# Attention: a batch is ranked two steps earlier in an even unit, and its fourth map scatter goes to an odd unit's fifth step

## The chip, the cores and the metric

The kernel runs on one core of a Trainium2 chip. The core has a tensor engine (PE; its weight loads are shown apart, as PEld), a vector engine (DVE), a scalar engine (ACT), a general engine (POOL) and a queue engine that issues transfers (SP). Each works through its own instructions in order, and they wait for one another by semaphores. The metric is the device time of one execution in microseconds.

## The reference, cut to what matters

```python
scores = cap * np.tanh(q @ k.T / sqrt(64) / cap)       # 8 batches, 12 heads, 448 x 448
attn   = exp(scores - max); attn /= attn.sum(-1)
x      = (attn @ v), heads side by side                # 3584 tokens x 768
logits = x @ w_gate + modality_bias[modality_id]       # 8 experts
e_idx  = argmax(logits); gate_w = softmax(logits)[e_idx]
out[t] = gate_w[t] * (relu(x[t] @ w1[e]) @ w2[e])      # e = e_idx[t]
```

Every token goes to one expert, so the tokens have to be sorted by expert between the two halves.

## The kernel before, in words

The attention is cut into 24 units `d`, each of four heads of one batch (three units make a batch). A unit has seven steps `s` of 64 keys, and the loop in `attention` goes through all 168 steps `n`. Each step puts these on the engines: four score products on PE (`scores`, line 542, `sc`), a tanh and, for two steps together, two exponentials on ACT (lines 547 and 549, `pt`), an add of the weights for the softmax's sums on DVE (`add`, line 562, `tot`), four steps behind, and the weighing of the values on PE (`weigh`, line 574, `xT`), four to six steps behind by a table. The last weighing of a unit falls into the fourth step of the next one, and a copy of `xT` on DVE follows it (`keep`, line 581).

For each pair of units, PE makes the logits in an even unit's sixth step (`sums2`, lines 613 and 615, `glog`) and transposes them in the next odd unit's fifth step (`turn2`, line 604, `lt`); DVE takes the reciprocals and scales the logits (lines 632 and 655). When a batch's three units are through, `route` ranks its 448 tokens: it is a Python generator cut by `yield`, which `start_route` starts in an odd unit's sixth step and `go_on` takes one piece further. Its pieces are:

- the sum of the logits (line 286), then the maximum and the one-hot choice `oh` (lines 294 to 313), in an odd unit's sixth and seventh step
- the running counts: three adds into `before` and one into `acc` (lines 319 and 320), and the gate (lines 300 to 302)
- the rank: two small products on PE, of `oh` (line 326) and of `before` (line 328), then five small DVE instructions to each token's row in a map (`rows`, `posf`, `pos`, lines 332 to 340), and scatters of the map's entries by POOL (line 346, `mapd`). For batches 0 to 4 only three of the four scatters are issued there; the fourth, with a cast of its own (line 360), is put into `self.rest` and issued later.

Instructions marked with `pin` keep the order in which the program writes them; the others of `route` are put in by a scheduler. The order that results is shown in the section on the change. After the attention, from about 300 us on, the experts' layers run, and PE works there without a break.

The calls that the change touches are these, in the loop of the steps:

```python
if s == 1 and d % 2 == 0 and self.rest:            # line 745: the fourth scatter
    self.rest.pop()()
if s in ((1,), (1, 6))[d % 2] and d != SOON + 2:   # line 747: a piece of route
    go_on()
...
for m in due[n]:                                   # line 764: the weighing of this step
    weigh(m)
...
if s == 3 and d % 2 == 0 and d != SOON + 2:        # line 768: a piece of route
    go_on()
```

Of the kernel before, what the change touches and what calls it, by code (L numbers as in the profile page):

```python
# [92 lines left out]
class Program:  # L93
# [414 lines left out]
    def attention(self, firsts, rp, xp):  # L508
        tc, nc = self.tc, self.nc
        pe, pin, V = nc.tensor, self.pin, nc.vector  # L510
        with ExitStack() as st:
# [10 lines left out]
            def fetch(d):  # L522
                if d < ND:
                    for g in (2 * d, 2 * d + 1) if d else ():
                        self.load_kq(ring[g % 4], g)
                    vas[d] = ld.tile([128, VW], F32, name="va")
                    self.load(vas[d], self.v[d // NU, d % NU])
# [6 lines left out]
            def scores(n):  # L534

                d, s = divmod(n, STEPS)
                sc = ps_s.tile([128, 2, 512], F32, name="sc")
                for i in range(2):
                    kq = ring[(2 * d + i) % 4]
                    for j in range(2):  # L540
                        rows = slice(j * D, (j + 1) * D)
                        pin(pe.matmul(  # L542
                            sc[i * KB : (i + 1) * KB, j, :S], kq[rows, S + s * KB : S + (s + 1) * KB], kq[rows, :S],
                            start=True, stop=True,
                        ))
                slow = n // STEPS == SOON + 2 and 2 <= n % STEPS <= 5
                pin(nc.scalar.activation(weights(n), sc[:, :, :S], AF.Tanh, scale=self.isc if slow else self.iscr))  # L547
                for m in (n - 1, n) if n % 2 else ():
                    pin(nc.scalar.activation(weights(m), weights(m), AF.Exp, scale=self.cabsr))  # L549
# [57 lines left out]
            def sums2(a, copy=V.tensor_copy):  # L607

                glog = self.glog = ps_g.tile([128, 512], F32, name="glog", tag="glog")
                group = lambda x: glog[x * GW : (x + 1) * GW, :S]  # L610
                every = [(u, g) for u in range(2) for g in range(2)]
                for u, g in every:
                    pin(pe.matmul(group(2 * u + g), self.pick2, tots[a + u][:, g], start=True, stop=False))
                for u, g in every:
                    pin(pe.matmul(
                        group(2 * u + g), self.wgt[:, (2 * (a + u) + g) % NP], kept[a + u][:, g], start=False, stop=True
                    ))
                gls[a] = xp.tile([128, S], F32, name="gl", bufs=2)
                pin(copy(gls[a], glog[:, :S]))
# [8 lines left out]
            def turn2(a):  # L628

                lt = flip(gls.pop(a))  # L630
                for u in range(2):
                    pin(V.reciprocal(recs(a + u), lt[:, :, 2 * u : 2 * u + 2, GE : GE + 2]))
                    lts[a + u] = lt[:, :, 2 * u : 2 * u + 2]
# [12 lines left out]
            def logits(d):  # L646

                b, r = divmod(d, NU)
                lt = lts.pop(d)
                rec = self.recips(pays[b])  # L650
                if r == 0:
                    lgs[b] = xp.tile([CP, C, H, E], F32, name="lg", bufs=2)
                for i in range(2):
                    h0 = 4 * r + 2 * i
                    pin(V.tensor_tensor(
                        lgs[b][:, :, h0 : h0 + 2], lt[:, :, i, :GE].rearrange("p c (j e) -> p c j e", j=2),
                        rec[:, :, :, 2 * r + i].unsqueeze(3).to_broadcast([CP, C, 2, E]), op=ALU.mult,
                    ))
# [10 lines left out]
            def store(b, queue=nc.sync):  # L669
                xs = xss.pop(b).rearrange("p m k b -> p m (k b)")  # L670
                wide = KC * HB
                for g in range(4):
                    j, h = divmod(g, 2)
                    o = (2 * h + j) * wide
                    put = queue.dma_start(
                        self.xd[b * S : (b + 1) * S, o : o + wide].rearrange("(m a) f -> a m f", a=HB),
                        xs[g * HB : (g + 1) * HB],
                    )
                    if queue is nc.sync:
                        self.last_sp = pin(put).ins  # L680
# [9 lines left out]
            def go_on():  # L690
                for way in routing:
                    next(way, None)
# [12 lines left out]
            SOON = (B - 1) * NU - 1  # L705
            END = STEPS * ND
            due = [[] for _ in range(END + 1)]
            for m in range(END):
                d, s = divmod(m, STEPS)
# [3 lines left out]
            def more(n, count=0):  # L713
                nonlocal added
                while (n not in held or count > 0) and added <= n - BEHIND + (n >= END - STEPS):
                    add(added)
                    added += 1
                    count -= 1
                    if count == 0:
                        break  # L720
# [3 lines left out]
            for n in range(END):  # L724
                d, s = divmod(n, STEPS)
                if s == 0:
                    fetch(d + 1)
                    if 1 < d < SOON and d % NU == 1:
                        store(d // NU - 1)
                    if d == 0:  # L730
                        self.fetch_bias()
                        self.fetch_cap()
                    if d == 1:
                        self.blank(xp.tile([128, FF], F32, name="spare", bufs=2))
                    if 0 <= d - 2 < CLEAR:
                        self.empty_map(d - 2)
                scores(n)
                late = False
                if not late:
                    more(n)  # L740
                if (d, s) == (1, 3):
                    self.gate_bias()
                if (d, s) == (1, 4):
                    self.columns()
                if s == 1 and d % 2 == 0 and self.rest:
                    self.rest.pop()()
                if s in ((1,), (1, 6))[d % 2] and d != SOON + 2:
                    go_on()
                if s == 4 and d % 2 and 3 <= d < PAIRED + 3:
                    turn2(d - 3)  # L750
                    go_on()
                    logits(d - 3)
                    logits(d - 2)
                if s == 5 and d % 2 == 0 and 2 <= d <= PAIRED:
                    sums2(d - 2)
                if (d, s) == (SOON + 1, 5):
                    sums(SOON)
                if s == 5 and d % 2 and 3 <= d < PAIRED + 2:
                    for u in (d - 3, d - 2):
                        if u % NU == NU - 1:  # L760
                            start_route(u // NU)
                if (d, s) == (SOON + 2, 2):
                    more(n, 1)
                for m in due[n]:
                    weigh(m)
                    if m % STEPS == STEPS - 1:
                        keep(m // STEPS)
                if s == 3 and d % 2 == 0 and d != SOON + 2:
                    go_on()
                if s == (2 if d % 2 else 4) and d % NU == 2:  # L770
                    tokens(d - 2)
                if s == (4 if d == SOON + 1 else 6) and 0 < d < ND - 1 and d % NU != 1:
                    tokens(d - 1)
                    if d == SOON + 1:
                        store(d // NU - 1)
                if d == SOON + 2 and s in (3, 4):
                    more(n, {3: 2, 4: 9}[s])
                if (d, s) == (SOON + 1, 6):
                    turn(SOON)
                    logits(SOON)  # L780
                    start_route(SOON // NU, firm=True)
                    go_on()
                    go_on()
                if (d, s) == (SOON + 2, 1):
                    go_on()
                    meta = self.early_slot(self.cpool, self.ps_r)
                    self.first_e = self.expert(meta, 0)
                    load_w1((0, 1), self.first_e)
                if (d, s) == (SOON + 2, 4):
                    maps = self.rows(meta, 0)  # L790
                    got = self.gather(maps, known=NT - S)
                    load_w1((2, 3, 4, 5), self.register(nc.gpsimd, meta[0:1, 0:1], E - 1, got.ins), nc.gpsimd)
                if d == SOON + 3 and s >= STEPS - TW:
                    self.norm(maps, s - (STEPS - TW))
# [818 lines left out]
```

## Time and profile before

| | us |
|---|---|
| median of three runs (lowest, highest) | 786.42 (786.34, 788.58) |
| profiled execution: time, and its span | 786.07, 784.5 |
| PE busy | 772.2 (98%) |
| PE weight loads busy | 580.0 (74%) |
| DVE busy | 524.3 (67%) |
| ACT busy | 500.0 (64%) |
| POOL busy | 238.4 (30%) |

The span goes from the first to the last instruction. A busy share is an average over two halves that differ: by the page's slices ACT is nearly full up to about 290 us and half idle after it, while PE is full in both. The trace splits each of PE's f32 products of 448 columns into two, so the four products of a step are eight there. A row of a timeline gives the start, the duration from the first of the merged instructions to the end of the last, the engine, line, tiles and count, and in brackets the engine's idle time before it and what ended that. Instructions of one engine overlap a little, so a row's end can lie behind the start of the next.

### The profile page before, as it was taken

The numbers are of one execution on the slowest core, as the hardware profiler recorded it, in microseconds if no ns is written. First come the engines' busy times: TensorE is split into PE (matmuls) and PEld (weight loads), VectorE is DVE, ScalarE is ACT, GpSimd is POOL, SyncE is SP. The second block draws the span as 40 slices with busy tenths as digits, with TensorE's granted clock in tenths as the row PEclk, the third lists the DMA queues.
The fourth block names the chain that finished last, engine by engine and source line by source line (L and its number), as shares of the span: only waits on it lengthen the run. The fifth ranks groups of instructions, "written<-read, shape, count | busy, mean of one in ns | idle before, by whom it ended". The sixth has DMA issues, their size and how long they took to land. (4 is left out here: it accounts for less than half of the span.)

```text
span 784.5 us, 15421 instructions
## 1 busy us (share of the span) xinstructions
PE 772.2 (98%) x5811; PEld 580.0 (74%) x5811; DVE 524.3 (67%) x899; ACT 500.0 (64%) x704; POOL 238.4 (30%) x259
## 2 busy tenths in 40 slices
PE   7999999999999999999999999999999999999996
PEld 2343333343333337999999999999999999998985
DVE  4778897888798898965826448265482664727830
ACT  7999999999999895454533445235443354436630
POOL 3000121022122140248560723607427064015202
PEclk9999999999999999999999999999999999999999
DMA  6366545262544664598444563455634655346772
GB/s 201 115 205 204 163 144 182 102 213 94 192 141 146 165 219 154 141 311 277 157 138 176 191 229 131 142 202 185 201 124 157 228 174 183 109 176 207 244 283 98
DMA packets 58951, 139.33 MB, mean 178 GB/s; under 512 B 9025, under 2 KB 25814, under 8 KB 58867
## 3 DMA queue, kind: packets, MB, share of 16 engines
q1 hardware_dynamic: 48512, 113.32, 44.3%
q0 software_dynamic: 10352, 24.94, 9.4%
q8 instruction: 47, 0.77, 0.4%
q14 instruction: 38, 0.30, 0.1%
q10 hardware_dynamic: 2, 0.00, 0.0%
HBM read 114.47 MB, written 24.34 MB: 177 GB/s over the span
## 5 line engine op out<-in xcount | busy, mean ns | idle before, releaser
L549 ACT ACTIVATE pt<-pt 128x896 f32<-128x896 f32 x168 | 152.2, 972 | 0.0
L547 ACT ACTIVATE pt<-sc 128x896 f32<-128x896 f32 x164 | 145.6, 938 | 9.9 <-PE sc L542 9.6
L574 PE MATMUL xT<-pt,va 64*64 64x448 f32 x1344 | 149.8, 537 | 0.1
L1111 PE MATMUL py<-bh,hh 128*128 128x384 f32 (+1 forms) x440 | 147.9, 336 | 0.1
L1111 PE MATMUL py<-bh,hl 128*128 128x384 f32 (+1 forms) x440 | 147.5, 335 | 0.0
L1111 PE MATMUL py<-bl,hh 128*128 128x384 f32 (+1 forms) x440 | 147.5, 335 | 0.0
L1054 PE MATMUL ph<-x,al 128*128 128x384 f32 (+1 forms) x456 | 147.3, 323 | 0.0
L957 POOL DMA_INDIRECT xg<-xd,at x92 | 112.3, 1221 | 112.1 <-DVE look L1275 85.0
L562 DVE TENSOR_TENSOR tot<-tot,pt 128x896 f32<-128x896 f32 x118 | 127.8, 1083 | 9.2 <-ACT pt L549 3.4
L1050 PE MATMUL ph<-x,ah 128*128 128x384 f32 x360 | 120.6, 335 | 0.0
L1051 PE MATMUL ph<-x,ah 128*128 128x384 f32 x360 | 120.3, 334 | 0.0
L346 POOL DMA_INDIRECT mapd<-pay,pos x32 | 39.8, 1245 | 244.7 <-DVE pos L340 128.6
L574 PEld LDWEIGHTS xT<-pt,va 64*64 64x64 f32 x1344 | 51.1, 133 | 75.5 <-issue 70.8
L995 DVE TENSOR_TENSOR bl<-raw,bh 128x768 fp32r<-128x768 f32 x78 | 72.2, 955 | 39.8 <-ACT bh L994 39.5
L1133 ACT ACTIVATE ot<-py,mt 128x384 f32<-128x384 f32 (+1 forms) x55 | 31.9, 581 | 104.7 <-PE py L1111 93.8
L1054 PEld LDWEIGHTS ph<-x,al 128*128 128x128 f32 x456 | 85.7, 188 | 0.0
L1065 ACT ACTIVATE hh<-ph 128x384 fp32r<-128x384 f32 x63 | 30.6, 489 | 84.9 <-PE ph L1054 80.7
L1111 PEld LDWEIGHTS py<-bh,hh 128*128 128x128 f32 x440 | 82.6, 188 | 1.2 <-ACT ot L1133 0.5
L1111 PEld LDWEIGHTS py<-bl,hh 128*128 128x128 f32 x440 | 82.6, 188 | 0.3
L1111 PEld LDWEIGHTS py<-bh,hl 128*128 128x128 f32 x440 | 82.6, 188 | 0.3
L542 PE MATMUL sc<-kq 64*64 64x448 f32 x672 | 78.3, 551 | 4.0 <-ACT pt L547 4.0
L542 PE MATMUL sc<-kx 64*64 64x448 f32 x672 | 78.5, 540 | 0.1
(245 smaller groups left out, 972.9 us busy)
## 6 DMA issues: line engine op xcount, KB each, us to landing
raw<-in_w_dram SPq DMA_DIRECT2D x81, 384.0 KB, 4.7
raw<-in_w_dram SPq DMA_DIRECT2D x48, 512.0 KB, 4.5
va<-in_v_dram SPq DMA_DIRECT2D x24, 448.0 KB, 5.7
kx<-in_kq_dram SPq DMA_DIRECT2D x24, 448.0 KB, 3.8
xd<-xs SPq DMA_DIRECT2D x32, 336.0 KB, 6.8
kq<-in_kq_dram SPq DMA_DIRECT2D x22, 448.0 KB, 4.0
raw<-in_w1q_dram SPq DMA_DIRECT2D x12, 512.0 KB, 7.6
mapd<-spare SPq DMA_DIRECT2D x4, 480.0 KB, 8.1
```

The source lines that it names most:

```text
L346: put = nc.gpsimd.indirect_dma_start(self.mapd, bass.IndirectOffsetOnAxis(ap=pos, axis=0), pay[:, c, :], None, bounds_check=E * RG - 1, oo ...
L542: pin(pe.matmul(sc[i * KB : (i + 1) * KB, j, :S], kq[rows, S + s * KB : S + (s + 1) * KB], kq[rows, :S], start=True, stop=True,))
L547: pin(nc.scalar.activation(weights(n), sc[:, :, :S], AF.Tanh, scale=self.isc if slow else self.iscr))
L549: pin(nc.scalar.activation(weights(m), weights(m), AF.Exp, scale=self.cabsr))
L562: pin(V.tensor_tensor(tots[d], pt_of(n - 1) if s == 1 else tots[d], pt_of(n), op=ALU.add))
L574: pin(pe.matmul(self.xT[j * D : (j + 1) * D, i, :S], vas[d][rows, o : o + D], pt[rows, j], start=s == 0, stop=s == STEPS - 1,))
L957: got = self.nc.gpsimd.indirect_dma_start(self.xg.rearrange("p t f -> p (t f)")[:, g * QW : (g + 1) * QW], None, self.xd.rearrange("n (q c ...
L995: keep((minus or self.nc.vector).tensor_tensor(lo, raw, hi, op=ALU.subtract))
L1050: keep(nc.tensor.matmul(ph[:, :w], hi[:, fs], self.x[:, k, 0, :w], start=first, stop=False))
L1051: keep(nc.tensor.matmul(ph[:, :w], hi[:, fs], self.x[:, k, 1, :w], start=False, stop=False))
L1054: self.done = keep(nc.tensor.matmul(ph[:, :w], lo[:, fs], self.x[:, k, 0, :w], start=False, stop=last)).ins
L1111: got = nc.tensor.matmul(pys[half][:, :wide], self.h[a][:, f, rows], self.w2s[f][c][:, cs], start=f == i == 0, stop=f == FC - 1 and i == 2,)
```

## The change

In an even unit, the piece of `route` that makes the counts is called in the first step in place of the second, and the piece that ranks is called in the second step, ahead of the weighing, in place of the fourth, behind it. The fourth scatter is issued in an odd unit's fifth step, ahead of the transposes' reciprocals, in place of an even unit's second.

```diff
-                if s == 1 and d % 2 == 0 and self.rest:
+                if s == 4 and d % 2 and self.rest:
                     self.rest.pop()()
-                if s in ((1,), (1, 6))[d % 2] and d != SOON + 2:
+                if s in ((0, 1), (1, 6))[d % 2] and d != SOON + 2:
                     go_on()
...
-                if s == 3 and d % 2 == 0 and d != SOON + 2:
-                    go_on()
```

Six batches are ranked there (0 to 5). On PE, batch 0's first four steps of the even unit stand like this before (`sc` are scores, `xT` the weighing; each row of scores or weighing is one step's four products, or two steps'):

```order
L542 MATMUL sc<-kq 64x448 x4
L574 MATMUL xT<-pt,va 64x448 x8
L542 MATMUL sc<-kq 64x448 x4
L574 MATMUL xT<-pt,va 64x448 x4
L542 MATMUL sc<-kq 64x448 x4
L574 MATMUL xT<-pt,va 64x448 x4
L326 LDWEIGHTS tri
L326 MATMUL rank<-oh,tri 112x32
L328 LDWEIGHTS ones
L328 MATMUL rank<-before,ones 112x32
L542 MATMUL sc<-kq 64x448 x8
```

The first row is the second step's scores. With the change, the same place of PE's order:

```order
L542 MATMUL sc<-kq 64x448 x4
L326 LDWEIGHTS tri
L326 MATMUL rank<-oh,tri 112x32
L328 LDWEIGHTS ones
L328 MATMUL rank<-before,ones 112x32
L574 MATMUL xT<-pt,va 64x448 x8
L542 MATMUL sc<-kq 64x448 x4
L574 MATMUL xT<-pt,va 64x448 x4
L542 MATMUL sc<-kq 64x448 x4
L574 MATMUL xT<-pt,va 64x448 x4
L542 MATMUL sc<-kq 64x448 x8
```

The rank has moved ahead of 16 weighing products and of two steps' scores. On DVE, from batch 0's `oh` on, before (`gs` and `pay` are the gate, `xs` the tokens' rows for the second half):

```order
L313 TENSOR_TENSOR oh<-sc,first 112x32
L665 STREAM_TRANSPOSE xs<-xT 128x14x64
L562 TENSOR_TENSOR tot<-tot,pt 128x896
L319 TENSOR_TENSOR before<-before,oh 112x8
L562 TENSOR_TENSOR tot<-tot,pt 128x896
L319 TENSOR_TENSOR before<-before,oh 112x8
L300 TENSOR_REDUCE gs<-ex 112x4
L319 TENSOR_TENSOR before<-before,oh 112x8
L301 TENSOR_SCALAR gs<-gs 112x4
L320 TENSOR_TENSOR acc<-before,oh 112x8
L302 RECIPROCAL pay_578<-gs 112x4
L562 TENSOR_TENSOR tot<-tot,pt 128x896 x2
```

And with the change:

```order
L313 TENSOR_TENSOR oh<-sc,first 112x32
L665 STREAM_TRANSPOSE xs<-xT 128x14x64
L562 TENSOR_TENSOR tot<-tot,pt 128x896
L319 TENSOR_TENSOR before<-before,oh 112x8 x3
L320 TENSOR_TENSOR acc<-before,oh 112x8
L300 TENSOR_REDUCE gs<-ex 112x4
L301 TENSOR_SCALAR gs<-gs 112x4
L302 RECIPROCAL pay_578<-gs 112x4
L562 TENSOR_TENSOR tot<-tot,pt 128x896
L332 TENSOR_TENSOR rows<-rank,region 112x32
L317 COPY before<-acc 112x8
L335 TENSOR_TENSOR rows<-rows,oh 112x32
```

Up to the first add into `before` nothing has moved; the three adds now stand together, and the rows behind the rank come ahead of two `tot` adds and the copy of `xT`. In batches 1, 3 and 5 the order is the same without the transposition of `xT` behind `oh`. ACT's and SP's instructions keep their order, and so do POOL's.

## Rows read from the trace of the kernel before

**Rows 1.** The page, busy time, share of the span and instructions of each engine.

```profile
PE 772.2 (98%) x5811; PEld 580.0 (74%) x5811; DVE 524.3 (67%) x899; ACT 500.0 (64%) x704; POOL 238.4 (30%) x259
```

**Rows 2.** Stretches: length; busy PE, PEld, DVE, ACT, POOL; clock, DMA share, GB/s.

```profile
47.84:71.44 23.60, 23.60 (x245) 9.10 (x245) 18.35 (x24) 23.24 (x29) 0.00 (x0) 1.00 0.69 218
71.44:95.40 23.96, 23.96 (x247) 9.18 (x247) 21.16 (x43) 23.37 (x30) 3.83 (x3) 1.00 0.50 160
...
214.47:238.43 23.96, 23.96 (x247) 9.17 (x247) 21.15 (x43) 23.37 (x29) 4.46 (x3) 1.00 0.51 161
```

**Rows 3.** ACT's waits, 70 to 250 us: total, times, longest.

```profile
ACT pt L547 <- PE sc L542: 4.0, 13, 0.4
```

**Rows 4.** The tile `rank`: count, shortest, median, longest ns, first and last start.

```profile
L328 PE MATMUL rank<-before,ones x7: 181/203/203, 81.9 to 315.2; 112*112 112x32 bf16 x7
```

**Rows 5.** PE's timeline, 72 to 92 us (batch 0's even unit).

```profile
77.20 1.69 PE L574 MATMUL xT<-pt,va 64*64 64x448 f32 x16
78.70 0.93 PE L542 MATMUL sc<-kq 64*64 64x448 f32 x8
...
80.96 0.93 PE L574 MATMUL xT<-pt,va 64*64 64x448 f32 x8
81.82 0.22 PE L326 MATMUL rank<-oh,tri 112*112 112x32 bf16 x1
81.89 0.20 PE L328 MATMUL rank<-before,ones 112*112 112x32 bf16 x1
82.02 1.73 PE L542 MATMUL sc<-kq 64*64 64x448 f32 x16
83.69 0.96 PE L613 MATMUL glog<-tot,pick 128*32 128x448 f32 x8
```

**Rows 6.** DVE's timeline, 72 to 92 us.

```profile
71.99 0.37 DVE L632 RECIPROCAL pay<-lt 112x16 f32<-112x16 f32 x2 [0.21 <-PE lt L604]
...
77.84 1.05 DVE L562 TENSOR_TENSOR tot<-tot,pt 128x896 f32<-128x896 f32 x1
78.81 0.15 DVE L319 TENSOR_TENSOR before<-before,oh 112x8 bf16<-112x8 bf16 x1
...
80.20 0.16 DVE L319 TENSOR_TENSOR before<-before,oh 112x8 bf16<-112x8 bf16 x1
...
80.39 0.16 DVE L320 TENSOR_TENSOR acc<-before,oh 112x8 bf16<-112x8 bf16 x1
```

**Rows 7.** All engines' timeline, 128 to 131 us (a unit without rank).

```profile
128.40 1.75 ACT L547 ACTIVATE pt<-sc 128x896 f32<-128x896 f32 x2
...
130.20 0.34 PEld L542 LDWEIGHTS sc<-kq 64*64 64x64 f32 x8 [0.41 <-ACT pt L547]
```

**Rows 8.** PE's timeline, 118 to 140 us (the same unit).

```profile
129.63 1.69 PE L542 MATMUL sc<-kq 64*64 64x448 f32 x16
131.25 0.96 PE L613 MATMUL glog<-tot,pick 128*32 128x448 f32 x8
```

**Rows 9.** All engines' timeline, 100.5 to 103.5 us (batch 1's even unit).

```profile
101.16 1.68 PE L574 MATMUL xT<-pt,va 64*64 64x448 f32 x16
...
101.78 0.16 DVE L319 TENSOR_TENSOR before<-before,oh 112x8 bf16<-112x8 bf16 x1
```

**Rows 10.** ACT's timeline, 80 to 92 us.

```profile
80.60 1.74 ACT L547 ACTIVATE pt<-sc 128x896 f32<-128x896 f32 x2
...
91.64 0.92 ACT L547 ACTIVATE pt<-sc 128x896 f32<-128x896 f32 x1 [0.23 <-PE sc L542]
```

**Rows 11.** Line 542's products: count, shortest, median, longest ns, first and last start.

```profile
L542 PE MATMUL sc<-kq x672: 535/536/1007, 4.6 to 278.4; 64*64 64x448 f32 x168
```

**Rows 12.** PE's timeline, 0 to 16 us.

```profile
10.89 1.79 PE L542 MATMUL sc<-kq 64*64 64x448 f32 x16 [1.50 <-ACT pt L547]
```

**Rows 13.** The first stretch, columns as in rows 2.

```profile
0.00:20.00 20.00, 15.35 (x121) 5.29 (x125) 9.41 (x22) 14.96 (x19) 6.97 (x29) 1.00 0.62 204
```

## The prediction

> **What bounds the kernel now.** The page comes first: the tensor engine (PE) is busy 772.2 of 784.5 us [rows 1]. That is an average, so the second view is the table of stretches, cut at the transposes that every odd unit of the attention makes (one stretch is two units, fourteen steps). PE is busy in all of it, 23.60 of 23.60 us where no batch is ranked and 23.96 of 23.96 where one is; ScalarE (ACT) is busy 23.24 and 23.37 [rows 2]. Of eight such stretches between 47.84 and 238.43 us, three have no rank and last 23.59 to 23.60, five have one and last 23.95 to 23.97. So a batch's two rank matmuls cost 0.36 us, at the place where they stand now. The third view is the waits of 70 to 250 us: PE waits for nobody there (that answer has no row for it), and ACT waits 13 times for scores, 4.0 us together [rows 3]. In the attention PE sets the pace, ACT has 1.5 to 2.5% to spare, and what is added to PE's chain comes out at the end unless PE had a gap to put it in.
>
> **The code.** Six batches (0 to 5) are moved. The trace has seven rank products in this tile, the seventh near 315 us being the last batch's [rows 4]; a batch between them uses another bank and path. PE, in program order, used to meet the rank behind the scores and the weighing of an even unit's fourth step; now it meets it right behind the scores of the second step, ahead of 16 weighing products and two more steps of scores (a step's four matmuls are eight in the trace). DVE's part moves one step too, but DVE comes to it by its own queue. The question is therefore when DVE has `before`, which the second rank product reads, and when PE stands there.
>
> **PE's arrival, even batches (0, 2, 4).** Batch 0: the scores of the second step are followed by weighing at 77.20 [rows 5]. This is where the rank would stand. Against the row before it, the switch from 64x64 products to the rank costs 0.11 us (weighing starts at 80.96; 16 products take 1.50 from 77.20 to 78.70, so eight take 0.75, which gives 81.71; the rank starts at 81.82). So the first rank product runs at 77.31; it needs only `oh`, long done.
>
> **DVE's readiness.** Up to the step in question DVE's order is unchanged: reciprocals, logits, the batch's reductions and `oh`, the transposition of xT, one tot add at 77.84, and the first `before` add at 78.81 [rows 6]. The reciprocal at 71.99 waits 0.21 for PE's transposes; none of DVE's rows from there to the add has an idle time ahead of it, so nothing can come sooner. Now the three adds stand in a row. Dependent small adds follow each other every 0.195 us (80.20 to 80.39), each 0.16 long, so the third ends at 78.81 + 2 x 0.195 + 0.16 = 79.36. A hand-over between engines I take as 0.05: a tanh group ends at 130.15 and PE's waiting weight load starts at 130.20 [rows 7]; that is another pair of engines, so it may be somewhat more here. The second rank product then starts at 79.41, and the next instruction 0.13 later (81.89 to 82.02), at 79.54. Without a rank, weighing would have begun at 77.20: PE is 2.34 late, plus 0.05 that the products behind a switch lose (82.02 to 83.69 is 1.67; in a pair without rank 129.63 to 131.25 is 1.62 [rows 8]). That is 2.39 in place of the present 0.36: **2.03 us more for an even batch.**
>
> **Odd batches (1, 3, 5).** No transposition of xT stands ahead. Batch 1: PE arrives at 101.16 and the first `before` add starts at 101.78 [rows 9]. Third add done at 102.33, product at 102.38, weighing at 102.51: 1.35 + 0.05 = 1.40, **1.04 us more than the 0.36 of today.**
>
> **What the other edits cost.** The cast and the fourth scatter of five batches go from an even unit's second step to an odd unit's fifth. There the cast stands ahead of the reciprocals, where DVE waits 0.21 for PE anyway [rows 6]; so I cost it at nothing; if that cover were gone it would be about 0.15 a batch, the length of a small add in the same rows, on DVE alone. POOL's order is the same and its scatters only come earlier. The five small DVE instructions behind the rank (rows, copy, product, reduction, cast, about 1 us at 0.195 each) now stand ahead of two tot adds and the copy of xT. The rank is ready by then (79.6, while DVE, with four small ones and a tot add of 0.97 behind 79.36, is at about 81), the copy has to wait for PE's last weighing product anyway, and PE needs it only for the second half of the glog products, which are 2.03 later too. Nothing is added there. Behind the rank, what is late next is ACT: the third step's scores now start at 78.70 + 2.39 = 81.09, end 0.93 later and let the tanh start at about 82.09 in place of 80.60 [rows 10], and the fourth's follow likewise. ACT then keeps up with PE to the next transposes, since its stall of 0.23 at 91.64 takes up the rest. PE's score buffers come free a little before PE needs them. So PE's delay passes on undivided.
>
> **Sum.** 3 x 2.03 + 3 x 1.04 = 9.2 us. Against the profiled execution (786.07, of which 784.5 is span) that is 795.3. The median of the runs shown is 0.35 above that execution; I forecast 795.4. Everything moved lies before 250 us and all later PE work hangs on it.
>
> **Bounds of what the trace does not show.** A PE that waits here for DVE is not in the trace. From above: if PE were released only behind the whole group that DVE issues there (accumulator, sum and gate: four instructions more, some 0.78 us by the spacing of the adds [rows 6]), six times 0.78 would be 4.7 more, 800.1. From below: if ACT were the true bound, the cost is what ACT starves, 82.09 - 80.60 = 1.49 in an even batch and, PE being 0.99 less late, 0.50 in an odd one: 6.0, 792.4 against the median. I take the value nearest to PE's rows.
>
> A rule that would put me on the lower end is in the Trainium skill, "Trainium Kernel Development and Optimization", section "Performance Expectations": matmul busy time is a bad metric, because matmuls are pipelined. By that rule PE's full rows prove nothing, and 792.4 would be the better sum. Here the 0.36 us between stretches with and without rank speaks against it [rows 2].
>
> **Rivals.**
> 1. ACT is the bound, PE's delay is partly hidden: 792.4. For it: ACT is busy 97 to 98% of each stretch. Against: two products on PE alone lengthen a stretch by 0.36.
> 2. The wait costs more. Either PE is released late (800.1), or the clock falls behind such a pause. Score products last 535 ns in general and up to 1007 ns at the start of the kernel [rows 11]; if the eight products behind each of six pauses ran at that pace, 0.75 us more each, the sum would be 4.5 higher, 799.9. Against: PE waits 1.50 us at 10.89 [rows 12] and the granted clock of the first 20 us is 1.00, its upper level, 2.4 GHz [rows 13]. The Trainium skill, "TensorE: Matmul & The Clock Gate", section "HAM oscillation — how this bites in real kernels", has it that waits between bursts can take the clock back to its lower level; the pause shown here did not do so.
> 3. The other side: DVE is ready when PE comes, the rank costs its 0.36 at either place, and ACT's stall of 0.23 at 91.64, taken for all six, goes: 786.4 - 6 x 0.23 = 785.0, or no change. The point from which it decides is `before` at 77.3 in even batches and 101.3 in odd ones, 2.1 and 1.1 us sooner than now. DVE has no idle time from the reciprocals on that it could be sooner by.
> 4. The rank does not really come sooner on PE: the order shows that it does. No change then.
>
> **How the numbers follow.** Forecast 0.82, with its own range 793.6 to 797.2 (0.3 us more or less in each of the six batches, for the hand-over and for ACT's margins). Rival 1 has 0.07, rival 2 0.05, rival 3 0.05, rival 4 0.01. The range for 8 in 10 or more reaches just below rival 1 and short of rival 2: 791.8 to 798.0. A measurement here tells 0.3%, about 2.4 us, from no change. Rivals 3 and 4 hold no change and faster: faster 0.02, within 0.3% 0.04, slower 0.94.
>
> **What would show it.** The rank's second product should wait for `before` (line 319), about 2.0 us in three batches and 1.0 in three; the stretches of rows 2 should last about 26.0 and 25.0 us where a batch is ranked and still 23.6 where none is; ACT should wait for the third step's scores by 1 to 1.5 us in even batches; the time behind 250 us should be unchanged but for a shift. I am wrong if PE shows no wait at the rank, if stretches with such a wait are not longer by it, or if those without a rank change.

## The result, and the profile after

The changed kernel takes 797.42 us (median of 6 runs, 795.43 to 798.44); the kernel before took 786.62 in the 6 runs beside it (786.34 to 788.58). The ratio is 1.0129, with a 95% interval of 1.0118 to 1.0140: slower by 10.8 us, where 9.0 were forecast (795.4).

The six times fall into two groups, and the mean granted clock of PE in the run (1.00 is full speed) goes with them: 795.43 and 795.58 at 0.998, and 797.35 to 798.44 at 0.994 to 0.996. The profiled execution, 797.8 us with a span of 796.2, is of the second group. So there are two questions: where the time common to all goes, and what happens in the second group.

The stretches of the changed kernel, cut at the same transposes; columns as in [rows 2].

```profile
48.18:71.78 23.60, 23.60 (x249) 9.07 (x245) 18.36 (x24) 23.24 (x28) 0.00 (x0) 1.00 0.69 218
71.78:97.74 25.96, 24.08 (x250) 9.17 (x247) 21.55 (x43) 23.59 (x29) 3.89 (x3) 1.00 0.47 149
97.74:122.70 24.96, 24.08 (x250) 9.17 (x246) 21.61 (x44) 23.59 (x29) 4.77 (x7) 1.00 0.38 126
...
146.30:173.97 27.67, 25.77 (x250) 9.70 (x246) 21.57 (x43) 23.59 (x29) 3.42 (x3) 0.94 0.44 140
...
222.54:248.54 26.00, 24.09 (x251) 9.16 (x247) 21.59 (x43) 23.59 (x29) 3.42 (x3) 1.00 0.46 148
```

The stretch without a rank is unchanged. Batches 0 and 4 cost 2.00 and 2.04 us more than the 23.96 of [rows 2], batch 1 costs 1.00. Batch 2, in the stretch from 146.30, costs 3.71, and the granted clock there is 0.94. All six together make 10.8 of the 11.7 us by which the span grew. The rest is 0.47 us ahead of the first of these transposes (at 48.18 us; at 47.71 before, where the cuts of [rows 2] lie 0.13 behind each group's start) and 0.45 behind the last; nothing that the change touches lies there.

PE's waits in the changed kernel from 70 to 260 us, total, times, longest; before, PE had none there.

```profile
PE rank L328 <- DVE before L319: 8.3, 6, 1.9
```

PE's timeline of batch 0's even unit, the counterpart of [rows 5].

```profile
76.92 0.93 PE L542 MATMUL sc<-kq 64*64 64x448 f32 x8
77.79 0.22 PE L326 MATMUL rank<-oh,tri 112*112 112x32 bf16 x1
79.89 0.18 PE L328 MATMUL rank<-before,ones 112*112 112x32 bf16 x1 [1.88 <-DVE before L319]
79.99 1.73 PE L574 MATMUL xT<-pt,va 64*64 64x448 f32 x16
81.55 0.93 PE L542 MATMUL sc<-kq 64*64 64x448 f32 x8
```

DVE's timeline at the same place, the counterpart of [rows 6].

```profile
78.32 1.05 DVE L562 TENSOR_TENSOR tot<-tot,pt 128x896 f32<-128x896 f32 x1
79.29 0.55 DVE L319 TENSOR_TENSOR before<-before,oh 112x8 bf16<-112x8 bf16 x3
79.87 0.16 DVE L320 TENSOR_TENSOR acc<-before,oh 112x8 bf16<-112x8 bf16 x1
```

The three adds stand together and end at 79.84, and the product that PE held back starts at 79.89, 0.05 later. It does not wait for the accumulator behind them, which starts at 79.87 and lasts 0.16. The 16 weighing products of the trace (eight in the program) start at 79.99; with no rank they would have stood about where the first rank product does.

ACT's timeline there, the third and the fourth step's tanh.

```profile
82.55 0.92 ACT L547 ACTIVATE pt<-sc 128x896 f32<-128x896 f32 x1 [1.34 <-PE sc L542]
84.05 0.92 ACT L547 ACTIVATE pt<-sc 128x896 f32<-128x896 f32 x1 [0.59 <-PE sc L542]
```

ACT starves, which costs nothing of its own: PE is the late one.

Batch 2 has the same wait, with another end. PE's timeline of the changed kernel, 150 to 175 us.

```profile
154.42 0.18 PE L328 MATMUL rank<-before,ones 112*112 112x32 bf16 x1 [1.90 <-DVE before L319]
154.53 2.89 PE L574 MATMUL xT<-pt,va 64*64 64x448 f32 x16
157.18 1.53 PE L542 MATMUL sc<-kq 64*64 64x448 f32 x8
158.53 0.93 PE L574 MATMUL xT<-pt,va 64*64 64x448 f32 x8
```

And the weight loads beside it.

```profile
155.69 0.26 PEld L574 LDWEIGHTS xT<-pt,va 64*64 64x64 f32 x4 [0.48 <-issue]
156.44 0.26 PEld L542 LDWEIGHTS sc<-kq 64*64 64x64 f32 x4 [0.48 <-issue]
158.53 0.15 PEld L574 LDWEIGHTS xT<-pt,va 64*64 64x64 f32 x4 [0.34 <-issue]
158.91 0.15 PEld L542 LDWEIGHTS sc<-kq 64*64 64x64 f32 x4 [0.22 <-issue]
```

Sixteen weighing products last 2.89 us in place of 1.73, eight score products 1.53 in place of 0.93; groups of four weight loads come every 0.75 us, and from 158.53 on about every 0.375 again. The granted clock of just this piece is in one row (columns as in [rows 2]):

```profile
154.53:158.53 4.00, 4.00 (x26) 1.50 (x28) 3.83 (x12) 1.20 (x2) 1.44 (x1) 0.57 0.04 14
```

From 154.90 to 158.30 alone the granted clock is 0.51, the lower of PE's two levels, 1.2 GHz. So behind this pause, and not behind those of batches 0 and 4, PE ran for about 3.4 us at half its speed. That costs batch 2 its 1.7 us over the 2.0 of its like (27.67 less the 25.96 and 26.00 of batches 0 and 4).

### The profile page after: what moved, and what is told of

Same layout as the page of the kernel before. It is cut to its first block, busy times and chain, and to the rows that moved or that the text cites. A ratio compares the mean times of both kernels' runs of the same rounds, so it can differ in the third digit from the quotient of the medians.

```text
span 796.2 us, 15415 instructions
## 1 busy us (share of the span) xinstructions
PE 775.6 (97%) x5811; PEld 580.7 (73%) x5811; DVE 526.1 (66%) x899; ACT 501.8 (63%) x704; POOL 232.8 (29%) x259
## 5 line engine op out<-in xcount | busy, mean ns | idle before, releaser
L955 POOL DMA_INDIRECT xg<-xd,at x92 | 110.7, 1203 | 114.6 <-DVE look L1273 87.5
L346 POOL DMA_INDIRECT mapd<-pay,pos x32 | 36.1, 1127 | 266.8 <-DVE pos L340 154.9
```

Of the source, the lines that this page charges most:

```text
L346: put = nc.gpsimd.indirect_dma_start(self.mapd, bass.IndirectOffsetOnAxis(ap=pos, axis=0), pay[:, c, :], None, bounds_check=E * RG - 1, oo ...
L955: got = self.nc.gpsimd.indirect_dma_start(self.xg.rearrange("p t f -> p (t f)")[:, g * QW : (g + 1) * QW], None, self.xd.rearrange("n (q c ...
```

## The experiments

**Which part of the change costs?** First the moved fourth scatter alone, with the rank left where it was (this edit and the next are against the kernel before):

```diff
-                if s == 1 and d % 2 == 0 and self.rest:
+                if s == 4 and d % 2 and self.rest:
```

> Only the fourth scatter and its cast move to an odd unit's fifth step; the rank stays behind the fourth step. Theory (PE waits at the rank for the running counts): nothing changes, 786.6, no PE wait, stretches with a rank 23.96. Rival (the cast ahead of the reciprocals or the earlier scatter costs part of the 10.8 us): 788 or more, and stretches longer than 23.96.

Measured: 786.46 us (11 runs; the kernel before, run beside it, 786.88), ratio 0.9994, interval 0.9985 to 1.0003. Its stretches are 23.60 and 23.96, as before:

```profile
71.63:95.59 23.96, 23.96 (x251) 9.18 (x247) 21.16 (x43) 23.38 (x29) 3.83 (x3) 1.00 0.48 159
```

Then the moved rank alone, with the scatter where it was:

```diff
-                if s in ((1,), (1, 6))[d % 2] and d != SOON + 2:
+                if s in ((0, 1), (1, 6))[d % 2] and d != SOON + 2:
...
-                if s == 3 and d % 2 == 0 and d != SOON + 2:
-                    go_on()
```

> Only the rank and the counts move; the fourth scatter stays in an even unit's second step. Theory: the whole loss, 795.4 to 798.4, stretches about 26.0 (even batches) and 25.0 (odd ones). Rival (scatter has a part): clearly below 795.

Measured: 795.33 us (4 runs; before 786.50), ratio 1.0120, interval 1.0096 to 1.0143. The profiled execution's stretches are 25.97, 25.98 and 25.98 for the even batches and 24.96 to 24.98 for the odd ones, all at clock 1.00:

```profile
145.50:171.48 25.98, 24.08 (x250) 9.16 (x246) 21.57 (x43) 23.59 (x29) 3.42 (x3) 1.00 0.47 150
```

This is batch 2, with the same 1.90 us wait that PE has in the changed kernel, and no fall of the clock. So the loss comes from the moved counts and rank alone, and the scatter has no part in it. One of the four runs took 797.88 us at a mean clock of 0.995.

**The same kernel again.** The changed kernel was run once more, unaltered, for the clock.

> The changed kernel once more, for the spread. Theory: 795.4 where the granted clock stays up in all stretches, and about 1.7 us more for each stretch in which it falls behind a wait of 1.9 us; such a fall only in the stretches of batches 0, 2 or 4, and not at the same batch in every execution. Rival (the 2 us between executions come from elsewhere, the start or the transfers): no stretch with a clock below 1.00 in a slow execution.

Measured: 796.92 us (4 runs: 794.97 and 795.72 at 0.999 and 0.998, 798.12 and 798.25 at 0.995 and 0.994), ratio 1.0134, interval 1.0108 to 1.0160. The profiled execution is the one of 795.72; its six stretches are 25.95, 24.97, 25.99, 24.97, 25.98 and 24.97, all at clock 1.00. Its span is 2.1 us below that of the first traced execution, and 1.68 of this lies in batch 2's stretch (25.99 against 27.67). This trace is of an execution without a fall, so by itself it does not decide between the theory and the rival. Over both times that the changed kernel ran and the kernel with the moved rank alone, 7 of 14 executions lie between 794.97 and 795.72 us, and 7 between 797.35 and 798.44, these at a mean clock of 0.994 to 0.996. Only one of these seven has a trace, and in it the clock fell behind one pause of three; that the other six have one or two such falls each is inferred from their time and mean clock.

**Does the loss follow the length of the wait?** Four kernels changed the wait. In the first, the counts are made one piece earlier, at the end of the odd unit, so that `before` is there almost when PE comes (this edit and those that follow are against the changed kernel, unless another is named):

```diff
-                if s in ((0, 1), (1, 6))[d % 2] and d != SOON + 2:
+                if s in ((1,), (1, 6))[d % 2] and d != SOON + 2:
                     go_on()
+                    if s == 6:
+                        go_on()
```

> The changed kernel, with the running counts made right behind the one-hot choice, in the odd unit's seventh step, so that DVE has them before its transposition and its next add. The rank stays where the change puts it. Theory: the counts are there about 0.2 us behind PE's arrival, the wait falls from 1.9 and 0.9 us to about 0.14 in all six batches, time 787.4 (786.6 if the wait goes wholly), no fall of the clock. Rival (the place itself costs: scores without weighing behind them, ACT starved in the third step): 793 or more, with no wait at the rank.

Measured: 789.50 us (5 runs; before 786.88), ratio 1.0035, interval 1.0022 to 1.0049. The odd batches came out as expected (24.09, 0.13 over the 23.96 of before), the even ones did not: 24.72 to 24.76. The time is 2.1 us over what was expected.

In the second the rank stands one step later, behind the third step's scores:

```diff
-                if s in ((0, 1), (1, 6))[d % 2] and d != SOON + 2:
+                if s in ((0, 2), (1, 6))[d % 2] and d != SOON + 2:
```

> The changed kernel with the rank behind the third step's scores, one step later. PE comes 1.5 us later in odd batches and 2.25 in even ones, DVE is the same. Theory: PE would be at the second product at 79.63 and the counts are ready at 79.41, so no wait, stretches 23.96, time 786.6. Rival (the cost lies in the small DVE instructions and the rank standing ahead of the copy of xT): still about half of the loss, 791.

Measured: 788.74 us (11 runs; before 786.88), ratio 1.0019, interval 1.0010 to 1.0028. PE no longer waits at the rank and odd batches are back at 23.96, but even ones last 24.49 to 24.51. The time is 2.1 us over what was expected here too. By their rows the two misses have one cause, which the matmuls' own row hides:

```profile
71.79:96.28 24.49, 24.49 (x250) 9.38 (x247) 21.48 (x43) 23.60 (x29) 3.94 (x3) 1.00 0.49 159
```

PE is "busy" for all of 24.49 us, yet there are as many products as ever. PE's timeline of this kernel shows the logits' second half lasting 1.47 us, where it took 0.94 before; the row before it is the first half. From the start of the first half to the scores behind them it is 2.18 us, in place of the 1.64 of before (83.69 to 85.33).

```profile
84.17 1.24 PE L613 MATMUL glog<-tot,pick 128*32 128x448 f32 x8
84.95 1.47 PE L615 MATMUL glog<-xT,wgt 128*32 128x448 f32 x8
86.35 0.98 PE L542 MATMUL sc<-kq 64*64 64x448 f32 x8
```

The weight loads of the same place name the waits:

```profile
84.47 0.14 PEld L613 LDWEIGHTS glog<-tot,pick 128*32 128x32 f32 x4 [0.15 <-DVE tot L562]
...
85.47 0.14 PEld L615 LDWEIGHTS glog<-xT,wgt 128*32 128x32 f32 x4 [0.40 <-DVE xT L581]
```

And DVE's timeline says why the `tot` add and the copy of `xT` are late: the small instructions behind the rank now stand ahead of them.

```profile
82.59 0.18 DVE L332 TENSOR_TENSOR rows<-rank,region 112x32 f32<-112x32 f32 x1
...
83.25 0.17 DVE L340 CAST pos<-posf 112x3 int32<-112x3 f32 x1
83.33 1.08 DVE L562 TENSOR_TENSOR tot<-tot,pt 128x896 f32<-128x896 f32 x1
84.33 1.08 DVE L581 COPY xT<-xT 128x896 f32<-128x896 f32 x1
```

In the kernel with early counts the same load waits 0.51 us for the copy. Odd batches have the same small instructions and the same copy, but no transposition of `xT` on DVE ahead of the counts. In batch 1 of the kernel with the rank in the third step the copy ends at 108.91, the first load for the logits' second half comes at 109.07 and does not wait, and there is no miss.

This reading was then put to the test by itself. Against the kernel with the rank in the third step, the four small instructions that read the rank (lines 332 to 340) were put behind the copy of `xT` and pinned there, and nothing else was moved. (The prediction counts five: the copy at line 317 stands among them, but makes the next batch's counts ready.) Three more `firmly` become `self.pin` in the same way:

```diff
+        if not firm:
+            yield
         rows = pool.tile([CP, C, E], F32, name="rows")
-        firmly(nc.vector.tensor_tensor(
+        self.pin(nc.vector.tensor_tensor(
...
+                if s == 3 and d % 2 == 0 and d != SOON + 2:
+                    go_on()
```

> The rank behind the third step's scores, as in the run before that kept 2 us of the loss, but with the four small DVE instructions that read it put behind the copy of xT. Theory (there the copy of xT came about 0.9 us later on DVE, behind those small instructions, and PE waited 0.5 us for it in the logits' products of even batches): stretches with a rank go from 24.50 back to 23.96 in even batches and stay 23.96 in odd ones; time equal to the kernel before. Rival (the 0.5 comes from the rank's place on PE): even stretches still 24.5, time 0.2% above the kernel before.

Measured: 786.19 us (11 runs; before 786.79), ratio 0.9995, interval 0.9986 to 1.0004. Even stretches are back at 23.96, and the logits' second half lasts 0.93 (line numbers are two higher in this kernel):

```profile
84.35 0.96 PE L615 MATMUL glog<-tot,pick 128*32 128x448 f32 x8
85.12 0.93 PE L617 MATMUL glog<-xT,wgt 128*32 128x448 f32 x8
```

So the order of DVE's small instructions costs 0.54 us per even batch as soon as the rank's wait no longer covers it. That this is also the miss of the kernel with early counts is read from its rows; there it was not put to the test. It is no part of the changed kernel's loss: there the copy starts at 84.80 and ends by 85.9, and PE, itself late, comes to the logits' second half at 86.94.

The third shortened the wait of even batches in another way: the transposition of `xT` on DVE, which stands between `oh` and the counts in even units only, goes behind them.

```diff
+                if s == 2 and d % 2 == 0 and d in (6, 12, 18):
+                    tokens(d - 2)
-                if s == (4 if d == SOON + 1 else 6) and 0 < d < ND - 1 and d % NU != 1:
+                if s == (4 if d == SOON + 1 else 6) and 0 < d < ND - 1 and d % NU != 1 and d not in (5, 11, 17):
```

> The changed kernel with DVE's transposition of xT (1.1 us) taken from ahead of the counts in batches 0, 2 and 4 and put into the even unit's third step. Theory: their wait falls from 1.9 to 0.9 us, all six stretches are about 25.0, time 786.6 + 6 x 1.0 = 792.7, and the clock stays up. Rival (the wait is not DVE's queue but the counts' own length or the hand-over): unchanged, 795.4 to 798.4.

Measured: 792.59 us (4 runs; before 786.50), ratio 1.0080, interval 1.0062 to 1.0098. All six stretches with a rank last 24.96 to 24.99, and batch 0 waits as an odd batch does:

```profile
78.01 0.18 PE L328 MATMUL rank<-before,ones 112*112 112x32 bf16 x1 [0.88 <-DVE before L319]
```

Six times 1.01 us is the 6.1 us of the time. One DVE instruction of 1.10 us makes the whole difference between an even and an odd batch. All six stretches stand at clock 1.00, and the mean clock is 0.997 to 0.999 in all four runs, as in the kernel before.

The fourth made the wait longer: counts and rank both come in the even unit's first step, so PE waits for `oh` as well.

```diff
-                if s in ((0, 1), (1, 6))[d % 2] and d != SOON + 2:
+                if s in ((0,), (1, 6))[d % 2] and d != SOON + 2:
                     go_on()
+                    if d % 2 == 0:
+                        go_on()
```

> The changed kernel with the rank already behind the first step's scores: PE comes 1.5 us sooner, DVE is the same. Theory: waits of about 3.4 and 2.4 us, stretches 27.5 and 26.5, 786.6 + 3 x 3.5 + 3 x 2.5 = 804.8 at full clock; if the clock falls behind long waits, about 1.7 us more for each fall, up to 815 with six. Rival (ACT is the bound and part is hidden): below 800.

Measured: 816.76 us (4 runs, 813.32 to 817.76; before 786.50), ratio 1.0369, interval 1.0340 to 1.0398. An even and an odd batch's stretch:

```profile
71.01:101.09 30.08, 26.72 (x251) 9.81 (x247) 21.65 (x43) 23.71 (x29) 3.79 (x3) 0.89 0.40 129
101.09:129.25 28.16, 25.80 (x250) 9.74 (x246) 21.70 (x44) 23.60 (x29) 4.78 (x7) 0.94 0.34 111
```

And PE's timeline of the even one:

```profile
76.66 0.18 PE L326 MATMUL rank<-oh,tri 112*112 112x32 bf16 x1 [1.08 <-DVE oh L313]
79.12 0.18 PE L328 MATMUL rank<-before,ones 112*112 112x32 bf16 x1 [2.28 <-DVE before L319]
79.23 1.77 PE L574 MATMUL xT<-pt,va 64*64 64x448 f32 x8
```

Batch 0 waits 1.08 and 2.28, batch 1 1.07 and 1.29. In the changed kernel a stretch grows by its wait and 0.12 (2.00 by a wait of 1.88, 1.00 by 0.88). By this the waits here cost 3.5 and 2.5 us; measured are 6.1 and 4.2. What is left, 2.6 and 1.7, goes with the clock: eight weighing products last 1.77 in place of 0.93, and the granted clock of all six stretches is down (0.89 three times, 0.94 three times), while the stretches between them last 23.59 to 23.60 at 1.00. In batch 0 the granted clock is down already within the second wait (0.68 from 76.90 to 79.12) and is 0.50 from there to 83.10. The 804.8 us expected for full clock are missed because the clock falls at every one of these pairs of waits in the profiled execution. The 815 for six falls are passed too, since a fall costs 2.6 in even batches where 1.7 was reckoned.

**Is there a better place for the rank?** Two kernels put it beside other products that leave the 64x64 shape, to save a switch. First right ahead of the logits' products:

```diff
-                if s in ((0, 1), (1, 6))[d % 2] and d != SOON + 2:
+                if s in ((0, 5), (1, 6))[d % 2] and d != SOON + 2:
```

> The changed kernel with the rank behind the sixth step's scores of an even unit, right ahead of the logits' products. Counts long ready, so no wait. Theory of the switch: both need the array's change from 64x64 products, and one change is saved, about 0.16 of the rank's 0.36 us: stretches with a rank about 23.8, time 785.6. Rival (nothing is saved): 23.96 and 786.6.

Measured: 786.40 us (11 runs; before 786.88), ratio 0.9994, interval 0.9985 to 1.0003. Odd stretches last 23.79 to 23.80, 0.16 less than before, as the saved switch would have it. Even ones last 23.87 to 23.89; their logits' second half takes 1.00 us, where it takes 0.94 in odd ones.

Then right behind them:

```diff
-                if s in ((0, 1), (1, 6))[d % 2] and d != SOON + 2:
+                if s in ((0,), (1, 6))[d % 2] and d != SOON + 2:
...
                     sums2(d - 2)
+                    go_on()
```

> The rank right behind the logits' products of the sixth step, with its DVE instructions behind the copy of the logits. Theory: one change of the array is saved as ahead of them, and nothing stands ahead of the copy of xT: stretches 23.80 in all six batches, 1.0 us less in all, 0.1% below the kernel before, which the comparison of times can just about tell. Rival (nothing saved here): 23.96 and the same time.

Measured: 786.27 us (11 runs; before 786.79), ratio 0.9996, interval 0.9987 to 1.0005. Odd stretches last 23.80, as expected, even ones 24.06 to 24.09, which was not. With the rank gone from ahead of them, the logits come sooner, and their second half runs into the copy of `xT`, which DVE starts at 82.66:

```profile
83.55 1.19 PE L615 MATMUL glog<-xT,wgt 128*32 128x448 f32 x8
```

1.19 us in place of 0.94 is 0.25 of the 0.26 to 0.29 by which even stretches are over the odd ones. That the copy, which ends at 83.74, is the reason is read from these times and was not tested apart. Neither version can be told from the kernel before, and no version tried beats it.

## Why the prediction was right, and where it was not

- **PE as the bound.** Right. Stretches grew by what PE waited and 0.12, while ACT's starving (1.34 and 0.59 us in the third and fourth step; forecast 1 to 1.5 for the third) changed nothing. The rival with ACT as the bound put 1.49 us on an even batch and 0.50 on an odd one; measured are 2.00 and 1.00.
- **The wait and its size.** Right. DVE's order up to the adds gave the moment at which `before` is there, the hand-over of 0.05 that was borrowed from another pair of engines held, and even and odd batches cost 2.00 and 1.00 where 2.03 and 1.04 stood. At full clock the six stretches grow by 9.07 in all (the second traced execution), against 9.2. Runs at full clock lie at 795 to 796 us, on the forecast. The forecast of 795.4 does not follow quite from its own sum, though: 786.42 and 9.2, or 795.3 and 0.35, make 795.6, and no reason for the 0.2 less is given.
- **The other edits at nothing.** Right for the cast and the scatter, shown by the kernel that moves them alone. For DVE's small instructions ahead of the copy of `xT`, "Nothing is added there" held only by the cover that the prediction named: PE's own lateness. Without it they cost 0.54 us an even batch, as the kernel that takes the wait away and the one that also moves them back show.
- **The clock, rival 2.** This is the step that failed: the forecast left the clock up behind the new waits. A fall had only part of rival 2's chance of 0.05, shared with a late release. By the times and mean clocks the fall happens in 7 of 14 executions, and it is why the median is 797.4 and not 795.4. Its price was put at 0.75 us for eight products behind each of six pauses. Where it comes it is 1.7 us: the products' pace was about right (up to 951 ns in place of 1007), but 24 pass through the fall and not eight. In the traced execution it comes behind one pause of three. The evidence against it was too weak for its chance: a wait of 1.50 us [rows 12], shorter than the 1.9 to come, and a granted clock of 1.00 averaged over 20 us [rows 13], in which score products also took 835 to 1007 ns (from 4.6 to 6.2 us). The Trainium skill, "TensorE: Matmul & The Clock Gate", section "HAM oscillation — how this bites in real kernels", says that waits between bursts can take the clock back to its lower level; one trace here agrees, with 0.57 behind batch 2's wait, and behind the eight other waits of this length the clock stays up.
- **The range.** 797.42 lies inside 791.8 to 798.0 by luck: that range was drawn to stop short of rival 2, and the forecast's own range, 793.6 to 797.2, is missed. Had more pauses been followed by a fall, the median would have left the wide range too, as three of the ten single runs of the changed kernel do (798.12 to 798.44).
- **The other half of rival 2**, a release only behind DVE's whole group, is out: the product starts 0.05 us behind the third add. Rivals 3 and 4, DVE ready in time and a rank no sooner on PE, are out by the same rows: the rank stands at 77.79, ahead of the weighing, and waits 1.88.
- **Time behind 250 us.** Unchanged but for the shift: 522.69 us from the last of these stretches to the end, 522.24 before (PE busy for 515.52 and 515.05 of them, so not wholly without a break).

What stays open is why one such pause is followed by the lower clock and the next is not: batch 2 itself shows no fall in the two other profiled executions, with pauses of 1.91 and 1.90 us, and no experiment was made on it. The length of the pauses alone does not sort the cases. At the start of the kernel before, PE pauses twice for 1.50 us, with 1.79 us of products between the pauses ([rows 12] and this row of the same timeline), and behind either the score products last 535 to 587 ns, which is full pace:

```profile
14.18 0.98 PE L542 MATMUL sc<-kq 64*64 64x448 f32 x8 [1.50 <-ACT pt L547]
```

Two pauses of 1.07 and 1.29 us with a single product of 0.18 us between them, in the kernel with the rank in the first step, are followed by a fall.

## What to carry to other kernels

Where the tensor engine sets the pace, as here, an instruction moved ahead on it can cost the whole time from its arrival to its operand's (2.00 us for a wait of 1.88); reckon both moments from the two engines' timelines, for each parity or variant of the loop apart. Then ask what the new lateness covers, since a second cost behind it shows only when the first is mended: look for it in the weight loads' rows, not in the matmuls'. A pause on the tensor engine has a price beyond its length, once the clock falls behind it; a chance for that must not rest on shorter pauses alone.

## What the runs showed of the hardware

- Pauses of 1.87 to 1.91 us on PE were followed by full clock in eight of nine cases in three profiled executions, and once by a granted clock of 0.57 for 4.00 us (0.51 for 3.40 of them). Behind pauses of 0.88 to 0.90 us no trace shows a fall. With two pauses on either side of one product of 0.18 us, 1.08 to 1.10 and 2.28 to 2.29 or 1.07 to 1.08 and 1.29, the clock was down in six stretches of six, in one profiled execution.
- A row of eight PE products can run on while a weight load among them waits for another engine: 1.47 us in place of 0.94, counted as busy, with the 0.40 us wait only in the row of the weight load. Single products there last 539 to 564 ns, 539 to 540 before.
- Two small products of another shape cost 0.36 us between 64x64 products [rows 2], and 0.20 beside others that already leave that shape (23.80 in place of 23.60).
